# Convolution, then a squared-ReLU MLP, on one core: the plain-float32 part run once per 24 steps instead of once per 16

## The chip, the core and the metric

One core of a Trainium2 chip runs the whole program. Five engines take part: TensorE (PE, with its weight loads as PEld), VectorE (DVE), ScalarE (ACT), GpSimd (POOL) and SyncE (SP), which here only issues DMA transfers. Each engine has its own instruction stream and works through it in the order of the program; semaphores hold an instruction back until what it needs has happened on another engine. The metric is device time in microseconds (us) of one execution. A difference of less than about 0.2% can't be told from no change with the runs made here.

## The reference: what is computed

Input x has 8 sequences of 4096 tokens with 192 features. The first stage is a causal convolution with 7 taps per head (8 heads of 24 features), its taps a softmax of `weight`. The second is an MLP on 32768 tokens:

```python
out = np.einsum('hk,bskhg->bshg', w, x_unf)     # 7 taps, w = softmax(weight)
h = x @ w_in                                    # 192 -> 2048
r = np.maximum(h, 0.0)
g = s * (r * r) + b
return (g @ w_out).astype(np.float32)           # 2048 -> 192
```

## The kernel before, in words

Features lie on partitions and tokens along the rows. The 192 features are split: **A** is features 0 to 127, **B** the last 64. Of B, two blocks of 512 tokens are stacked on the 128 partitions.

**Tokens and steps.** Tokens go in groups of 1024, numbered n = 0 to 31; a group has two blocks j of 512. The hidden layer's 2048 units are 8 pairs p of 2x128. A *step* (n, j, p) computes one pair for one block. There are 512 steps, 16 per group; n = 0 and 1 run an older scheme (`OLD = 2`), the 480 steps of n = 2 to 31 the one that matters here.

**What a step does.** `first` (L549) makes h in PSUM: each operand is split into a high part of few bits and the rest, and three of the four products are taken, 18 matmuls of 64 rows, of which two run side by side on the two halves of the array. ACT applies Relu (L572) and Square (L580), which leaves the squares q in SBUF in float32. DVE makes the high part qh (L582) and the rest ql (L586). Two steps later (`LAG = 2`, the list `queue`) `second` (L717) multiplies qh and ql by the A columns of `w_out`, 12 matmuls, and accumulates over the 8 pairs. h has two buffers: the `first` of a step needs the Relu of the step two before.

**Features B.** The 64 B columns of the output are not made from qh and ql. The squares q are kept (`kept`, a ring of tiles named q), and once per group a *batch* makes them in plain float32: `second_B` (L736) runs, for each of the two blocks of the group before, 8 pairs x 4 matmuls of 64 rows and 64 columns, which run four at a time. The page counts each of them as two. After each block `evict_B` takes the result out:

```python
nc.scalar.activation(o, accs[0], ..., scale=sb, bias=...)       # L746, ACT, into oB
nc.scalar.activation(o2, accs[1], ..., scale=sb)                # L747, ACT, into oB2
nc.gpsimd.tensor_tensor(o, o, o2, op=ALU.add)                   # L748, POOL: first add
nc.sync.dma_start(oC, o[DB:P])                                  # L749, SP: upper half down
nc.gpsimd.tensor_tensor(oC, oC, o[0:DB], op=ALU.add)            # L750, POOL: second add
nc.sync.dma_start(outT[P:D, t0 : t0 + BLK], oC)                 # L751, SP: to HBM
```

The second add reads the lower half of oB; only after it may oB be written again. The tile `outs` has nine places: oA and oB rotate through three places each, oC, oB2 and oA2 have one. A is taken out likewise (L724 to L727), once per block.

**The convolution.** DVE does it for the group ahead, 7 instructions per piece of 128x512 (L174 and six times L176) for A of block 0, A of block 1 and B. `split_A` then makes the high part on ACT (L191), the rest on DVE (L193), and swaps the two 64-partition halves with two DMAs (L184, L185). `split_B` needs five DVE instructions and the same two DMAs. These are laid out as a stream of parts; `convolve(k)` puts the next k parts at its place in the program. Inputs of a group are loaded by two DMAs (xB L160, xA L163) into two buffers in turn; in the program they stand where the buffer's last reader has been issued, and the DMA waits on SP until that reader is done.

**What sets the order.** DVE, ACT and PE are held to the order in which the code issues them (`in_order`). SP and POOL too work through their streams in the order in which they stand in the program. So where a waiting DMA stands on SP, all DMAs behind it wait as well.

Of the kernel before, what the change touches and what calls it, by code (L numbers as in the profile page):

```python
# [17 lines left out]
P = 128  # L18
# [11 lines left out]
RING = 18  # L30

GAP = 40

FIRST = (3, 4, 2, 7)
# [11 lines left out]
def conv_attention_then_squared_relu_mlp(  # L46
# [96 lines left out]
    class Tokens:  # L143
        def __init__(self, n):
            self.n = n
            self.sA, self.wA = {}, {}
            self.todo = self.steps() if n else iter(())

            self.begun = False

        def load(self):
            n = self.n
            t0 = n * SUP
            self.xA = xin.tile([P, PAD + SUP], F32, name="xA")
            self.xB = xin.tile([P, PAD + BLK], F32, name="xB")
# [4 lines left out]
            nc.sync.dma_start(self.xB, xB[n])  # L160
            x0 = t0 - PAD
            cut = PAD + BLK if n == 0 else PAD + SUP
            nc.sync.dma_start(self.xA[:, skip:cut], xA[:, x0 + skip : x0 + cut])  # L163
            if n == 0:
                fetch(0, 0, CI)
                nc.sync.dma_start(self.xA[:, cut:], xA[:, BLK:SUP])

        def conv(self, acc, x, w, width):


            for k in range(K):
                src = x[:, k : k + width]
                if k == 0:
                    nc.vector.tensor_scalar(acc, src, w[:, 0:1], None, op0=ALU.mult)  # L174
                else:
                    nc.vector.scalar_tensor_tensor(  # L176
                        acc, src, w[:, k : k + 1], acc, op0=ALU.mult, op1=ALU.add
                    )
                yield k == K - 1
# [7 lines left out]
        def split_A(self, j, acc):  # L187

            s = self.sA[j] = xs.tile([P, 2, BLK], F32R, name="sA", bufs=3)
            self.wA[j] = xs.tile([P, 2, BLK], F32R, name="wA", bufs=3)  # L190
            nc.scalar.copy(s[:, 0, :], acc)  # L191
            yield
# [3 lines left out]
            self.swap(self.wA[j], s)  # L196
            yield

        def split_B(self, acc):

            self.tB = xs.tile([P, 2, BLK], F32R, name="tB")
            self.wB = xs.tile([P, 2, BLK], F32R, name="wB")
            hiB = xs.tile([P, BLK], F32R, name="hiB", bufs=1)
            nc.vector.tensor_copy(hiB, acc)
            yield
            for j in range(2):
                r = slice(j * DB, (j + 1) * DB)
                nc.vector.tensor_copy(self.tB[0:DB, j, :], acc[r, :])
                nc.vector.tensor_tensor(
                    self.tB[DB:P, j, :], acc[r, :], hiB[r, :].bitcast(F32), op=ALU.subtract  # L210
                )
                if j == 1:
                    self.swap(self.wB, self.tB)
                    self.begun = True
                yield

        def split_B_at_once(self, acc):

            self.tB = xs.tile([P, 2, BLK], F32R, name="tB")
            self.wB = xs.tile([P, 2, BLK], F32R, name="wB")  # L220
            hiB = xs.tile([P, BLK], F32R, name="hiB", bufs=1)
            nc.scalar.copy(hiB, acc)
            for j in range(2):
                r = slice(j * DB, (j + 1) * DB)
                places = (self.tB, self.wB) if j == 0 else (self.tB,)
                for k, to in enumerate(places):
                    nc.scalar.copy(to[k * DB :][0:DB, j, :], hiB[r, :].bitcast(F32))
                for k, to in enumerate(places):
                    nc.vector.tensor_tensor(
                        to[(1 - k) * DB :][0:DB, j, :], acc[r, :], hiB[r, :].bitcast(F32),  # L230
                        op=ALU.subtract,
                    )
                if j == 1:
                    self.swap(self.wB[:, 1, :], self.tB[:, 1, :])
                self.begun = True
                yield
# [9 lines left out]
        def half(self, j, i):  # L246
# [3 lines left out]
            b = (self.tB, self.wB) if i == 0 else (self.wB, self.tB)  # L250
# [3 lines left out]
                (2, b[0][r, j, :], b[1][r, j, :]),  # L254
            )

        def steps(self):
            for j in range(2):
                acc = xs.tile([P, BLK], F32, name="accA")
                yield from self.conv(acc, self.xA[:, j * BLK :], tapA, BLK)  # L260
                yield from self.split_A(j, acc)
                if j == 0:
                    acc = xs.tile([P, BLK], F32, name="accB", bufs=1)
                    yield from self.conv(acc, self.xB, tapB, BLK)
                    yield from (self.split_B_at_once if self.n == 1 else self.split_B)(acc)
# [7 lines left out]

        def finish(self, block):
            while not (block == 0 and self.begun) and next(self.todo, self) is not self:
                pass

# [80 lines left out]
    def fetch(p, a=0, z=None):  # L358
        if a == 0:
            k = 3 * (p % 3)  # L360
            room = outs[:, k : k + 3, :].rearrange("p a b -> p (a b)").bitcast(I32)
            words[p] = room.rearrange("p (f w) -> p f w", w=2)
# [5 lines left out]
    def room_for(dtype):  # L368
        return act.tile([P, 2, BLK], dtype, name="q")

    raw = [room_for(I32).rearrange("p a b -> p (a b)")[:, 0:CT] for _ in range(3)]
    splitB = [
        room_for(F32R).rearrange("p a (f k d) -> p (a f) k d", k=2, d=DB) for _ in range(2)
    ]
    scratch = room_for(F32)
    idle, ident = (scratch[:, k, 0:P] for k in range(2))
# [25 lines left out]
    def head():  # L402
# [11 lines left out]
        def diagonal(w):  # L414
            d = room_for(F32).rearrange("p a (k f) -> p (a k) f", f=P)
# [5 lines left out]
        diagB = diagonal(tapB)  # L421
# [3 lines left out]
        acc0 = xs.tile([P, BLK], F32, name="accA")  # L425
# [3 lines left out]
        diagA = diagonal(tapA)  # L429
        w0.magnitudes()  # L430
        split = one.split_A(0, acc0)
# [3 lines left out]
        tB = one.tB = xs.tile([P, 2, BLK], F32R, name="tB")  # L435
        wB = one.wB = xs.tile([P, 2, BLK], F32R, name="wB")
        hiB = xs.tile([P, BLK], F32R, name="hiB", bufs=1)
        lo = one.split_tensor(accB, hiB, lambda: one.conv_tensor(acc1, diagA, one.xA[:, BLK:], range(0, 2)))
# [6 lines left out]
        nc.scalar.copy(tB[top, 0, :], hiB[top].bitcast(F32))  # L445
        nc.scalar.copy(wB[bottom, 0, :], hiB[top].bitcast(F32))
        lo(tB[bottom, 0, :], top)
        lo(wB[top, 0, :], top)
# [5 lines left out]
        nc.scalar.copy(tB[top, 1, :], hiB[bottom].bitcast(F32))  # L454

        def second_block():
            sA = one.sA[1] = xs.tile([P, 2, BLK], F32R, name="sA", bufs=3)
            wA = one.wA[1] = xs.tile([P, 2, BLK], F32R, name="wA", bufs=3)
            lo1 = one.split_tensor(acc1, sA[:, 0, :])
            one.swap(wA[:, 0, :], sA[:, 0, :])  # L460
            lo(tB[bottom, 1, :], bottom)
            one.swap(wB[:, 1, :], tB[:, 1, :])
# [11 lines left out]
        start_tokens(1)  # L474
# [87 lines left out]

    def split_place(g):
        if g < OLD * 2 * NPAIR + LAG + 2 and g % DEEP > LAG:
            return room_for(F32R), room_for(F32R)
# [56 lines left out]
    def second_whole(n, j, p, qh, ql):  # L622
# [17 lines left out]
        if p == NPAIR - 1:  # L640
            t0 = n * SUP + j * BLK
            oA = out_tile("oA")
# [3 lines left out]
            oB = out_tile("oB")[0:DB]  # L646
# [7 lines left out]
    def second_split(n, j, p, qh, ql):  # L654
# [19 lines left out]
        if p == NPAIR - 1:  # L674
# [3 lines left out]
            o = {}  # L678
            own = None if early else room_for(F32)
            for k, name in ((1, "oB"), (0, "oA")):  # L680
                o[k] = out_tile(name) if early else own[:, k, :]
# [101 lines left out]
    def start_tokens(n):  # L783
        if n < NSUP:
            tok[n] = Tokens(n)
            tok[n].load()

    queue = []

    coming = [1]  # L790
# [3 lines left out]
    def convolve(k):  # L794


        k += owed[0]
        while k and coming[0] in tok:
            try:
                stop = next(tok[coming[0]].todo)  # L800
            except StopIteration:
                coming[0] += 1
                continue
            k -= 1
            if stop:
                break
        owed[0] = k if coming[0] in tok else 0
# [47 lines left out]
    steps = [(n, j, p) for n in range(NSUP) for j in range(2) for p in range(NPAIR)]  # L855

    def step(n, j, p):
        if p == 0:
            tok[n].finish(j)
            if j == 0:  # L860
                with headed():
                    start_tokens(n + 1)
            else:
                tok.pop(n - 1)
# [92 lines left out]
```

## Time and profile before

| what | value |
|---|---|
| median of 3 runs (lowest, highest) | 2223.55 us (2223.49, 2223.86) |
| profiled execution, its own time | 2223.51 us |
| its span from first to last instruction | 2221.7 us |
| PE busy / PEld busy | 2216.5 us (100%) / 1608.4 us (72%) |
| DVE busy / ACT busy / POOL busy | 1738.7 us (78%) / 1318.2 us (59%) / 302.6 us (14%) |
| granted PE clock | 1.00 |

The profile is of one execution, which took 1.8 us more than its span. A row of a timeline has the start in us from the span's start, the length, the engine, the line, what it writes and reads, its shape, and in brackets how long the engine stood idle before it and what ended that. "SPq" is the issue of a DMA, its landing comes later. A busy PE says little here, since matmuls overlap; the distance from one start to the next tells its pace.

### The profile page before, as it was taken

The numbers are of one execution on the slowest core, as the hardware profiler recorded it, in microseconds if no ns is written. First come the engines' busy times: TensorE is split into PE (matmuls) and PEld (weight loads), VectorE is DVE, ScalarE is ACT, GpSimd is POOL, SyncE is SP. The second block draws the span as 40 slices with busy tenths as digits, with TensorE's granted clock in tenths as the row PEclk, the third lists the DMA queues.
The fourth block names the chain that finished last, engine by engine and source line by source line (L and its number), as shares of the span: only waits on it lengthen the run. The fifth ranks groups of instructions, "written<-read, shape, count | busy, mean of one in ns | idle before, by whom it ended". The sixth has DMA issues, their size and how long they took to land.

```text
span 2221.7 us, 44630 instructions
## 1 busy us (share of the span) xinstructions
PE 2216.5 (100%) x19334; PEld 1608.4 (72%) x19334; DVE 1738.7 (78%) x1980; ACT 1318.2 (59%) x1424; POOL 302.6 (14%) x199
## 2 busy tenths in 40 slices
PE   9999999999999999999999999999999999999999
PEld 6788777777777777777877777777777777777776
DVE  8898787787877878778787777887787877878754
ACT  8758555566555665555655556555566555665554
POOL 0001111111111011111111101111111111011110
PEclk9999999999999999999999999999999999999999
DMA  5113212112121121211111111112112121121110
GB/s 181 33 34 95 57 48 61 48 47 58 44 58 48 44 58 44 58 51 51 48 54 49 53 50 47 53 49 63 46 46 58 44 58 49 46 56 39 44 30 17
DMA packets 46165, 117.49 MB, mean 53 GB/s; under 512 B 7760, under 2 KB 8016, under 8 KB 45968
## 3 DMA queue, kind: packets, MB, share of 16 engines
q1 hardware_dynamic: 45824, 114.50, 18.6%
q8 instruction: 151, 2.47, 0.5%
q14 instruction: 46, 0.38, 0.1%
q10 hardware_dynamic: 144, 0.13, 0.0%
HBM read 31.64 MB, written 25.17 MB: 26 GB/s over the span
## 4 chain that ended last, share of the span: by engine, by line
PE 98%; ACT 1%; DVE 1%; issue 0%; DVEq 0%; POOL 0%; POOLq 0%
PE h L549 47%; PE acc L717 29%; PE acc L736 18%; PE acc L661 2%; PE acc L270 1%; PE h L736 0%; ACT q L580 0%; PE acc L631 0%; PE acc L637 0%; PE acc L639 0%; PE acc L638 0%; ACT q L572 0%; PE acc L409 0%; DVE ql L586 0%; PE acc L630 0%; PE acc L633 0%
## 5 line engine op out<-in xcount | busy, mean ns | idle before, releaser
L572 ACT ACTIVATE q<-h 128x1024 f32<-128x1024 f32 x512 | 526.2, 1028 | 563.7 <-PE h L549 561.6
L586 DVE TENSOR_TENSOR ql<-q,qh 128x1024 fp32r<-128x1024 f32 x498 | 668.1, 1342 | 57.0 <-ACT qh L582 5.5
L582 DVE CAST qh<-q 128x1024 fp32r<-128x1024 f32 x482 | 342.5, 711 | 360.1 <-ACT q L580 356.3
L717 PE MATMUL acc<-qh,W 64*128 64x512 f32 x3816 | 588.1, 386 | 0.0
L580 ACT ACTIVATE q<-q 128x1024 f32<-128x1024 f32 x512 | 543.6, 1062 | 16.0
L549 PE MATMUL h<-sA,W 64*128 64x512 f32 x3072 | 436.1, 389 | 0.0
L549 PE MATMUL h<-wA,W 64*128 64x512 f32 x3072 | 431.9, 386 | 0.0
L549 PE MATMUL h<-wB,W 64*128 64x512 f32 x1536 | 430.3, 386 | 0.0
L549 PE MATMUL h<-tB,W 64*128 64x512 f32 x1536 | 430.3, 386 | 0.0
L717 PEld LDWEIGHTS acc<-qh,W 64*128 64x128 f32 x3816 | 357.4, 184 | 76.2 <-issue 0.8
L736 PE MATMUL acc<-q,WB 64*64 64x512 f32 x3776 | 412.1, 591 | 0.0
L717 PE MATMUL acc<-ql,W 64*128 64x512 f32 x1908 | 371.4, 386 | 0.0
L549 PEld LDWEIGHTS h<-sA,W 64*128 64x128 f32 x3072 | 285.1, 184 | 84.1 <-issue 24.7
L549 PEld LDWEIGHTS h<-wA,W 64*128 64x128 f32 x3072 | 287.8, 184 | 60.8
L736 PEld LDWEIGHTS acc<-q,WB 64*64 64x64 f32 x3776 | 141.5, 133 | 254.7 <-issue 254.7
L176 DVE SCALAR_TENSOR_TENSOR accA<-xA,tap,accA 128x512 f32<-128x512 f32 x378 | 312.9, 828 | 5.7
L549 PEld LDWEIGHTS h<-tB,W 64*128 64x128 f32 x1536 | 282.5, 184 | 41.1 <-issue 0.2
L549 PEld LDWEIGHTS h<-wB,W 64*128 64x128 f32 x1536 | 282.5, 184 | 20.4
L726 POOL TENSOR_TENSOR outs<-outs 128x512 f32<-128x512 f32 x59 | 95.4, 1617 | 1225.7 <-ACT outs L725 1225.7
L717 PEld LDWEIGHTS acc<-ql,W 64*128 64x128 f32 x1908 | 178.7, 184 | 37.7
L176 DVE SCALAR_TENSOR_TENSOR accB<-xB,tap,accB 128x512 f32<-128x512 f32 x186 | 167.5, 900 | 6.3
L748 POOL TENSOR_TENSOR outs<-outs 128x512 f32<-128x512 f32 x59 | 107.1, 1816 | 199.7 <-ACT outs L747 199.4
(146 smaller groups left out, 888.4 us busy)
## 6 DMA issues: line engine op xcount, KB each, us to landing
wA<-sA SPq DMA_DIRECT2D x126, 256.0 KB, 3.6
outT<-outs SPq DMA_DIRECT2D x62, 256.0 KB, 2.0
wB<-tB SPq DMA_DIRECT2D x60, 256.0 KB, 3.4
xA<-in_xA SPq DMA_DIRECT2D x24, 515.0 KB, 3.6
outT<-outs SPq DMA_DIRECT2D x65, 128.0 KB, 2.3
xB<-in_xB SPq DMA_DIRECT2D x32, 259.0 KB, 3.0
outs<-outs SPq DMA_DIRECT2D x60, 128.0 KB, 2.7
outs<-in_w SPq DMA_DIRECT2D x7, 768.0 KB, 6.1
```

The source lines that it names most:

```text
L176: nc.vector.scalar_tensor_tensor(acc, src, w[:, k : k + 1], acc, op0=ALU.mult, op1=ALU.add)
L270: nc.tensor.matmul(acc, diag[:, k, :], x[:, k : k + BLK], start=k == 0, stop=k == K - 1)
L549: nc.tensor.matmul(h[:, i, :], w_in(w, p, chunk[0], rows), chunk[part], start=start, stop=stop)
L572: nc.scalar.activation(q, h, AF.Relu)
L580: nc.scalar.activation(q, q, AF.Square)
L582: cast(qh, q)
L586: nc.vector.tensor_tensor(ql, q, qh.bitcast(F32), op=ALU.subtract)
L661: nc.tensor.matmul(accs[to + 2 * i][0:cols], w(f, r), q[r, f % 2, :], start=start and f == 0, stop=stop and f == NF - 1,)
L717: nc.tensor.matmul(accs[i], w(f, r), q[r, f % 2, :], start=f == 0 and lo == 0, stop=f == ends[i] and lo == 2,)
L726: nc.gpsimd.tensor_tensor(o, o, o2, op=ALU.add)
L736: nc.tensor.matmul(accs[r.start // HB][i * DB : (i + 1) * DB], WB[r, p, i, :], q[r, i, :], start=p == 0, stop=p == NPAIR - 1, skip_group_c ...
L748: nc.gpsimd.tensor_tensor(o, o, o2, op=ALU.add)
```

## The change

What it does, part by part:

- **Batches.** B is made once per 24 steps, three blocks at a time (`batch(k)`, `WINDOW`). 19 batches and three blocks in the last step take the place of 29 batches and two blocks in the last step. A batch stands at the second step of its 24 (`edge == 1`). At the first (`edge == 0`) the step's Relu is put off; Relu, Square, qh and ql of both steps come just ahead of the batch.
- **The ring of squares** is 12 tiles of two steps each (24 squares), before 18 tiles of one. The first Relu at a batch writes into a tile that the batch's first two pairs must have been read from.
- **SBUF.** To make room, `outs` has five places: oA, oB, oC, oB2 and oA2 have one each, none rotates. xA and xB have one buffer each, before two. The weights' staging area at the start lies in the ring.
- **B split as A.** `split` replaces `split_A` and `split_B`: one ACT and one DVE instruction for B too, and the halves' roles in `half` follow.
- **The convolution** is one stream (`pieces`) in the order B, A0, A1 per group. A split waits (`gated`) until the steps that read the buffer before it have been issued. One part per step goes in, 7 at edge 0, none at edge 1, and 5, 5 and 4 in the batch's three blocks. The next group's xB and xA are loaded right where the last tap of the present one is issued.

The order on three engines' queues at a batch, as the program has it. `Pool_49`, `PE_49`, `DVE_49` and `Activation_49` are the semaphores that POOL, PE, DVE and ACT raise, `DMAHW..` those of DMAs.

ACT before, from the Relu of the batch's step to that of the next (L724 and L725 take out A, L191 is a part of the convolution, L746 and L747 take out the two B blocks):

```order
L572 ACTIVATE q<-h 128x1024 [waits PE_49]
L580 ACTIVATE q<-q 128x1024 [waits Activation_49]
L724 ACTIVATE outs<-acc_9727,bias,sb 128x512 [waits DMAHW0_49,PE_49]
L725 ACTIVATE outs<-acc_9728,sb 128x512 [waits PE_49,Pool_49]
L191 CAST sA<-accA 128x512 [waits DMAHW3_49,DMAHW2_49,DVE_49]
L746 ACTIVATE outs<-acc_10030,bias,sb 128x512 [waits DMAHW4_49,PE_49]
L747 ACTIVATE outs<-acc_10031,sb 128x512 [waits PE_49]
L746 ACTIVATE outs<-acc_10076,bias,sb 128x512 [waits DMAHW0_49,PE_49]
L747 ACTIVATE outs<-acc_10077,sb 128x512 [waits PE_49,Pool_49]
L572 ACTIVATE q<-h 128x1024 [waits PE_49]
```

ACT in the changed kernel, the same place (L707 and L708 take out A, L555 is Relu, L563 Square, L214 a part of the convolution, L729 and L730 take out the three B blocks):

```order
L707 ACTIVATE outs<-acc_9138,bias,sb 128x512 [waits DMAHW6_49,PE_49,Pool_49]
L708 ACTIVATE outs<-acc_9139,sb 128x512 [waits PE_49]
L555 ACTIVATE q<-h 128x1024 [waits PE_49]
L563 ACTIVATE q<-q 128x1024 [waits Activation_49]
L555 ACTIVATE q<-h 128x1024
L563 ACTIVATE q<-q 128x1024 [waits Activation_49]
L214 CAST sA<-acc 128x512 [waits DMAHW4_49,DMAHW3_49,DVE_49]
L729 ACTIVATE outs<-acc_9439,bias,sb 128x512 [waits DMAHW0_49,PE_49]
L730 ACTIVATE outs<-acc_9440,sb 128x512 [waits PE_49]
L729 ACTIVATE outs<-acc_9487,bias,sb 128x512 [waits DMAHW0_49,PE_49,Pool_49]
L730 ACTIVATE outs<-acc_9488,sb 128x512 [waits PE_49,Activation_49]
L729 ACTIVATE outs<-acc_9532,bias,sb 128x512 [waits DMAHW2_49,PE_49,Pool_49]
```

The L729 of the second and third block now waits for `Pool_49`, which it did not before: the count that it waits for is that of the second add (now L733) of the block ahead of it, since oB has one place. Behind the third block's pair stands the next step's Relu.

SP before, at a batch (L184 and L185 swap the halves of a convolved block, L160 loads xB, L749 and L751 belong to the two B blocks):

```order
L184 DMA wA<-sA 64x1024 [waits DMAHW3_49,DVE_49,PE_49]
L185 DMA wA<-sA 64x1024 [waits DMAHW4_49]
L160 DMA xB<-in_xB 128x518 [waits DMAHW5_49,DVE_49]
L749 DMA outs<-outs 64x512 [waits DMAHW6_49,Pool_49]
L751 DMA outT<-outs 64x512 [waits DMAHW7_49,Pool_49]
L749 DMA outs<-outs 64x512 [waits DMAHW7_49,DMAHW0_49,Pool_49]
L751 DMA outT<-outs 64x512 [waits DMAHW1_49,Pool_49]
```

SP in the changed kernel at an odd batch (the first, third and so on; L190 and L191 swap, L168 loads xA, L732 and L734 belong to the B blocks):

```order
L190 DMA wA<-sA 64x1024 [waits DMAHW5_49,DVE_49,PE_49]
L191 DMA wA<-sA 64x1024 [waits DMAHW6_49]
L168 DMA xA<-in_xA 128x1030 [waits DMAHW7_49,DVE_49]
L732 DMA outs<-outs 64x512 [waits DMAHW0_49,Pool_49]
L734 DMA outT<-outs 64x512 [waits DMAHW1_49,Pool_49]
L732 DMA outs<-outs 64x512 [waits DMAHW2_49,DMAHW1_49,Pool_49]
L734 DMA outT<-outs 64x512 [waits DMAHW3_49,Pool_49]
L732 DMA outs<-outs 64x512 [waits DMAHW4_49,DMAHW3_49,Pool_49]
```

and at an even one (L172 loads xB):

```order
L172 DMA xB<-in_xB 128x518 [waits DMAHW3_49,DVE_49]
L732 DMA outs<-outs 64x512 [waits DMAHW4_49,Pool_49]
L734 DMA outT<-outs 64x512 [waits DMAHW5_49,Pool_49]
L732 DMA outs<-outs 64x512 [waits DMAHW6_49,DMAHW5_49,Pool_49]
L190 DMA wB<-sB 64x1024 [waits DMAHW7_49,DVE_49]
L191 DMA wB<-sB 64x1024 [waits DMAHW0_49]
L734 DMA outT<-outs 64x512 [waits DMAHW1_49,Pool_49]
L732 DMA outs<-outs 64x512 [waits DMAHW2_49,DMAHW1_49,Pool_49]
```

An input's load still stands ahead of the first block's downward DMA (L749 before, L732 now), in batches 1 to 18; in odd ones it is now xA, in even ones xB. In batch 19 nothing is left to load. On DVE, qh and ql of the two put-off steps stand ahead of the batch's parts; the load waits for the seventh tap of a block behind them: in odd batches seven taps and one split come between, in even ones six taps.

The core of the diff:

```diff
-RING = 18
+RING = 12
+BATCH = 24
+WINDOW = (5, 5, 4)
-FIRST = (3, 4, 2, 7)
...
-    outs = wide_w.tile([P, 9, BLK], F32, name="outs")
+    outs = wide_w.tile([P, 5, BLK], F32, name="outs")
-    xin = ctx.enter_context(tc.tile_pool(name="xin", bufs=2))
+    xin = ctx.enter_context(tc.tile_pool(name="xin", bufs=1))
...
+        def split(self, kind, j, acc):
+            s, w = self.places(kind, j)
+            nc.scalar.copy(s[:, 0, :], acc)
             yield
+            self.lo(s, acc)
+            self.swap(w, s)
             yield
...
     def room_for(dtype):
-        return act.tile([P, 2, BLK], dtype, name="q")
+        return act.tile([P, 2, 2, BLK], dtype, name="q")
...
     def relu(h):
         g = count[0]
         count[0] += 1
-        q = room_for(F32)
+        if g % 2 == 0:
+            two[0] = room_for(F32)
+        q = two[0][:, g % 2]
         nc.scalar.activation(q, h, AF.Relu)
         return q, g
...
-    room = {"oA": 0, "oB": 3, "oC": 6, "oB2": 7, "oA2": 8}
-    turn = {"oA": 0, "oB": 0}
+    room = {"oA": 0, "oB": 1, "oC": 2, "oB2": 3, "oA2": 4}
     def out_tile(name):
-        k = room[name]
-        if name in turn:
-            k += turn[name]
-            turn[name] = (turn[name] + 1) % 3
-        return outs[:, k, :]
+        return outs[:, room[name], :]
...
+    def pieces():
+        def whole(n, kind, j):
+            t = tok.setdefault(n, Tokens(n))
+            acc = xs.tile([P, BLK], F32, name="acc")
+            x = t.xB if kind == "B" else t.xA[:, j * BLK :]
+            for k, _ in enumerate(t.conv(acc, x, tapB if kind == "B" else tapA, BLK)):
+                if k < K - 1:
+                    yield None
+            with headed():
+                if kind == "B" and n + 1 < NSUP:
+                    tok[n + 1] = Tokens(n + 1)
+                    tok[n + 1].load_B()
+                elif j == 1 and n + 1 < NSUP:
+                    tok[n + 1].load_A(PAD + SUP)
+            yield "tapped"
+            gate = 16 * n - (0 if j else 8 if kind == "A" else 16)
+            while n + j > 1 and now[0] < gate:
+                yield "gated"
+            once = (n, kind) == (1, "B")
+            split = t.split_B_at_once(acc) if once else t.split(kind, j, acc)
+            next(split)
+            yield "after" if once else "cast"
+            next(split)
+            ready.add((n, kind, j))
+            yield None
...
-    def batch(n):
-        a = second_B(n, 0, banks())
-        convolve(FIRST[2])
-        evict_B(n, 0, a)
-        a = second_B(n, 1, banks())
-        convolve(FIRST[3])
-        evict_B(n, 1, a)
+    def batch(k):
+        for b, parts in zip(range(3 * k - 3, 3 * k), WINDOW):
+            block = OLD + b // 2, b % 2
+            a = second_B(*block, banks())
+            convolve(parts)
+            evict_B(*block, a)
+    def pace(g):
+        return 0 if g % BATCH < 2 else 1
...
+        g = now[0] - 16 * OLD
         h = first(n, j, p)
+        edge = g % BATCH if g >= BATCH else BATCH
+        if edge == 0:
+            convolve(4)
+            convolve(3)
+            second(*queue.pop(0))
+            waiting.append((n, j, p, h))
+            return
+        if edge == 1:
+            second(*queue.pop(0))
+            *at, before = waiting.pop()
+            put(*at, squares(before, nc.vector.tensor_copy))
...
         if (n, j, p) == steps[-1]:
-            a = second_B(n, 0, banks())
-            h = ps_h.tile([P, 2, BLK], F32, name="h")
-            b = second_B(n, 1, [h[:, i, :] for i in range(2)])
-            evict_B(n, 0, a)
-            last_B(n, 1, b)
+            a = second_B(n - 1, 1, banks())
+            evict_B(n - 1, 1, a)
+            for i in range(2):
+                h = ps_h.tile([P, 2, BLK], F32, name="h")
+                a = second_B(n, i, [h[:, k, :] for k in range(2)])
+                (last_B if i else evict_B)(n, i, a)
...
-        if n > OLD and (j, p) == (0, 1):
-            batch(n - 1)
+        if edge == 1:
+            batch(g // BATCH)
```

More of the change, by code (lines that the diff above doesn't have):

```diff
@@ L185, in swap, with places, lo @@
             nc.sync.dma_start(to[HB:P], of[0:HB])
[L187 to L192, printed above, removed]
+        def places(self, kind, j=0):
+            if (self.n, kind, j) == (0, "A", 0):
+                room = room_for(F32R)
+                s, w = room[:, 0], room[:, 1]
+            else:
+                s, w = (xs.tile([P, 2, BLK], F32R, name=x + kind) for x in "sw")
+            if kind == "A":
+                self.sA[j], self.wA[j] = s, w
+            else:
+                self.sB, self.wB = s, w
+            return s, w
+        def lo(self, s, acc):
             nc.vector.tensor_tensor(
@@ L217, in split_B_at_once @@
-        def split_B_at_once(self, acc):
[L219 to L236, printed above, removed]
+            self.lo(s, acc)
@@ L253, in half @@
                 (1 - i, self.wA[j][r, 0, :], self.wA[j][r, 1, :]),
-                (2, b[0][r, j, :], b[1][r, j, :]),
+                (2, b[r, 0, :], b[r, 1, :]),
             )
[L257 to L265, printed above, removed]
         def conv_tensor(self, acc, diag, x, taps=range(K)):
@@ L424, in head @@
         one.conv_tensor(accB, diagB, one.xB)
-        acc0 = xs.tile([P, BLK], F32, name="accA")
+        acc0 = xs.tile([P, BLK], F32, name="acc")
         for _ in one.conv(acc0, one.xA, tapA, BLK):
@@ L434, in head @@
         w0.his()
[L435 to L438, printed above, removed]
+        sB, wB = one.places("B")
+        lo = one.split_tensor(accB, sB[:, 0, :], lambda: one.conv_tensor(acc1, diagA, one.xA[:, BLK:], range(0, 2)))
         one.conv_tensor(acc1, diagA, one.xA[:, BLK:], range(2, K))
@@ L781, in last @@
             e.dma_start(outT[0:P, t0 + c.start : t0 + c.stop], oA[:, c])
[L783 to L786, printed above, removed]
     queue = []
-    coming = [1]
+    now = [0]
+    def pieces():
[23 more added lines that the diff above has]
+            yield None
+        order = [(1, "A", 0), (1, "B", 0), (1, "A", 1)]
+        for n in range(2, NSUP):
+            order += [(n, "B", 0), (n, "A", 0), (n, "A", 1)]
+        todo = [whole(*c) for c in order]
+        ahead = False
+        while todo:
+            said = next(todo[0], "over")
+            if said == "over":
+                todo.pop(0)
+                ahead = False
+                continue
+            if said in ("cast", "gated") and len(todo) > 1 and not ahead:
+                if said == "cast":
+                    yield said
+                said = next(todo[1])
+                ahead = said == "tapped"
+            yield said
+    ready = set()
+    stream = pieces()
     owed = [0]
@@ L797, in convolve, with need @@
         k += owed[0]
[L798 to L803, printed above, removed]
-            k -= 1
-            if stop:
-                break
-        owed[0] = k if coming[0] in tok else 0
+        owed[0] = 0
+        while k > 0:
+            said = next(stream, "over")
+            if said in ("over", "gated"):
+                return
+            k -= 1
+            if said == "tapped":
+                owed[0] = k
+                return
+    def need(*what):
+        while what not in ready:
+            if next(stream) == "gated":
+                raise ValueError(what)
     def pair(p):
@@ L873, in step @@
         else:
-            convolve(FIRST[p] if j == 0 and p < 2 else 1)
+            convolve(pace(g))
         if (n, j, p) == (2, 0, 0):
```

131 lines of the change are left out of this document (68 added, 63 removed).

## The prediction

> **What bounds the kernel now.** The page first: busy shares, then the chain of work that ended last.
>
> ```profile
> PE 2216.5 (100%) x19334; PEld 1608.4 (72%) x19334; DVE 1738.7 (78%) x1980; ACT 1318.2 (59%) x1424; POOL 302.6 (14%) x199
> ...
> PE 98%; ACT 1%; DVE 1%; issue 0%; DVEq 0%; POOL 0%; POOLq 0%
> ```
>
> PE is never free, and the chain is PE's own work to 98%. Everything else lies beside it. So a change can gain only by giving PE less time per token, and lose only by making PE wait. The pieces of that chain in order of time show the batches (first, a neighbour, the last with the two blocks of the last step):
>
> ```profile
> 905.06 13.89 PE acc L736 x128
> 973.62 13.89 PE acc L736 x128
> ...
> 2199.53 7.03 PE acc L736 x64
> 2206.56 6.87 PE h L736 x64
> ```
>
> A group of 16 steps takes 973.62 - 905.06 = 68.56 us. A block of B takes 6.87 (the second of the last step), and 0.16 more when it follows a step. Three stages, the batch, the step after it and the next one:
>
> ```profile
> 973.62:987.44 13.82, 13.82 (x128) 4.72 (x129) 12.71 (x15) 3.92 (x6) 2.97 (x2) 1.00 0.20 58
> 987.44:991.01 3.57, 3.57 (x34) 2.92 (x32) 1.03 (x2) 2.49 (x4) 0.00 (x0) 1.00 0.39 105
> 991.01:994.41 3.40, 3.40 (x32) 2.81 (x30) 2.31 (x2) 2.08 (x3) 2.19 (x2) 1.00 0.02 7
> ```
>
> An ordinary step is 3.40 us; the first after a batch is 3.57. 16 x 3.40 + 2 x 6.87 = 68.14, and 68.56 - 68.14 = **0.42 us is what one change to plain float32 and back costs**. PE has no other slack per group, and its clock stands at 1.00.
>
> **The change part by part.**
>
> *Fewer batches.* 29 batches become 19, the blocks stay 60: 10 x 0.42 = **-4.2 us**. The blocks in the last step are three and not two; the third moved there, its 6.87 us is in the sum anyway.
>
> *B split as A, one stream of parts, the new head.* Four DVE instructions fewer per group and one on ACT instead; they lie under PE. Cost 0, and no gain. One cover is thin: before every even batch a block's halves are swapped some 1.7 steps ahead of use. By my count of its Relu, Square, qh, ql and split its DMAs land about 0.2 us ahead of their matmuls; a late landing costs up to 1 us there. I take 0.
>
> *oB with one place.* This is where I expect the loss. How a block of B leaves the core, in the batch at 973.55, ACT, then SP, POOL and DVE:
>
> ```profile
> 981.67 0.77 ACT L746 ACTIVATE outs<-acc,bias,sb 128x512 f32<-128x512 f32 x1
> 982.35 0.68 ACT L747 ACTIVATE outs<-acc,sb 128x512 f32<-128x512 f32 x1
> 987.55 0.78 ACT L746 ACTIVATE outs<-acc,bias,sb 128x512 f32<-128x512 f32 x1 [4.52 <-PE acc L736]
> ...
> 989.85 1.03 ACT L572 ACTIVATE q<-h 128x1024 f32<-128x1024 f32 x1 [0.94 <-PE h L549]
> 990.91 1.06 ACT L580 ACTIVATE q<-q 128x1024 f32<-128x1024 f32 x1
> ```
> ```profile
> 988.53 0.33 SPq L160 DMA_DIRECT2D xB<-in_xB  x1
> 988.96 0.46 SPq L749 DMA_DIRECT2D outs<-outs  x1
> ```
> ```profile
> 983.10 1.70 POOL L748 TENSOR_TENSOR outs<-outs 128x512 f32<-128x512 f32 x1 [6.09 <-ACT outs L747]
> 992.22 1.62 POOL L750 TENSOR_TENSOR outs<-outs 64x512 f32<-64x512 f32 x1 [7.42 <-DMA outs<-outs]
> ```
> ```profile
> 981.80 0.69 DVE L193 TENSOR_TENSOR sA<-accA,sA 128x512 fp32r<-128x512 f32 x1 [0.68 <-ACT sA L191]
> 982.41 0.48 DVE L174 TENSOR_SCALAR accB<-xB,tap 128x512 f32<-128x512 f32 x1
> 982.92 5.58 DVE L176 SCALAR_TENSOR_TENSOR accB<-xB,tap,accB 128x512 f32<-128x512 f32 x6
> ```
>
> From L746 to the end of the second add, 993.84 - 981.67 = 12.17 us. The first add was done at 984.80, but its downward DMA went out at 988.96: on SP it stood behind the load of xB, which waited for DVE's last tap (982.92 + 5.58 = 988.50). In a batch with nothing to load, and at the very end, the same way is short:
>
> ```profile
> 2010.07 0.77 ACT L746 ACTIVATE outs<-acc,bias,sb 128x512 f32<-128x512 f32 x1
> ...
> 2015.75 1.51 POOL L750 TENSOR_TENSOR outs<-outs 64x512 f32<-64x512 f32 x1 [2.55 <-DMA outs<-outs]
> ```
> ```profile
> 2206.60 0.78 ACT L746 ACTIVATE outs<-acc,bias,sb 128x512 f32<-128x512 f32 x1 [4.90 <-PE acc L736]
> ...
> 2211.67 1.26 POOL L750 TENSOR_TENSOR outs<-outs 64x512 f32<-64x512 f32 x1 [2.37 <-DMA outs<-outs]
> ```
>
> 7.19 and 6.33 us. Before, the second block's L746 ran at 987.55 as soon as PE had the block, since oB rotated. Now it waits for the first block's second add, the third's for the second's, and behind the third on ACT stands the next Relu, for which PE waits. The places beside:
>
> ```profile
> 970.05 0.84 PE L549 MATMUL h<-sA,W 64*128 64x512 f32 x6
> ...
> 972.09 0.62 PE L717 MATMUL acc<-qh,W 64*128 64x512 f32 x4
> 972.55 0.39 PE L717 MATMUL acc<-ql,W 64*128 64x512 f32 x2
> ```
> ```profile
> 1009.01 0.69 DVE L582 CAST qh<-q 128x1024 fp32r<-128x1024 f32 x1 [0.31 <-ACT q L580]
> 1009.81 1.23 DVE L586 TENSOR_TENSOR ql<-q,qh 128x1024 fp32r<-128x1024 f32 x1
> ```
> ```profile
> xA<-in_xA SPq DMA_DIRECT2D x24, 515.0 KB, 3.6
> ...
> xB<-in_xB SPq DMA_DIRECT2D x32, 259.0 KB, 3.0
> ```
> ```profile
> DMA to landing us min/median/max: 2.2/2.6/4.9
> ```
>
> (The last row is that of L749.) Now a clock that starts with a batch's first float32 matmul, for the changed kernel:
>
> - The put-off Relu needs the tile of the first two pairs: 4 groups of four matmuls, 6.87/16 = 0.43 each, about 2.0. Relu, Square, Relu, Square: 2 x (1.03 + 1.06), to 6.1. DVE's qh and ql of the second: 0.69 + 1.23 and some 0.15 of gaps, to 8.2.
> - *Odd batches*: first tap 0.48, split 0.69, six taps 5.58 (with POOL's first add in them, as in the row): 14.9. xA's load goes out, L732 0.43 later (988.53 to 988.96). The add followed that by 3.26; xA is twice xB and lands 0.6 later: 3.9. The add itself, DVE soon idle, 1.4. The first block is out at 20.6.
> - *Even batches*: only six taps, 13.8; behind xB 0.43 + 3.3 + 1.4: 18.9.
> - The second block starts there (PE had it at 14.0) and takes 6.33 to 7.19; I take 6.8 in odd batches, and 7.2 in even ones, where taps and a swap run beside it. The third starts at 27.4 and 26.1. Its two ACT instructions take 1.36, the next Relu 1.03: done at **29.8 and 28.5**.
> - What PE needs: three blocks end at 0.15 + 20.61 = 20.76 on this clock (987.44 - 973.55 is 0.15 over two blocks), steps of 3.57 and 3.40 follow, so the third `first`, which needs that Relu's buffer, is due at 27.7, its `second` 2.04 and the first ql 2.50 later: 30.2. From the Relu's end to ql's end: 1.06 + 0.69 + 1.23 + gaps = 3.1. The Relu must end by **27.1**.
> - So PE loses 29.8 - 27.1 = 2.7 us in an odd batch, 1.4 in an even one, in two waits (first h, then ql). Batches 1 to 18: 9 x 2.7 + 9 x 1.4 = **+36.9**. Batch 19 has no load: twice 7.2 from 7.1 is 21.5, in time; 0.
>
> Sum: -4.2 + 36.9 = +32.7. The profiled execution took 2223.51 for a span of 2221.7, 0.04 from the median of 2223.55: **2256 us**.
>
> Bounds of the loss, which the trace of before doesn't contain. From below: taps without POOL's share (about 0.9 less), landings of 2.2, adds of 1.26 and second blocks of 6.33 give 26.6 in odd batches: nothing lost, -4.2 in all. From above: a landing of 4.9 and the second block at 7.6 (a slower add than 1.51) make some 4.4 and 3.0: +67. I stay near the middle, since the row behind a load (3.26) is the nearest there is.
>
> The Trainium skill ("DMA: Bandwidth & Descriptors", Issuing engines are not separate DMA queues) says that starting DMAs from several engines saves only the time to initiate them, small beside the transfer. By it the place behind a load on SP would cost 0.4 us, the first block would be out at about 14.5, and the sum would be -4.2. The row above disagrees: 4.16 us between the first add's end and its DMA, a wait of the issuing engine and no transfer.
>
> **The rivals.**
>
> - *A: the way out stays hidden* (not slower). If the first block is out by 18, or a short way makes up for it, the third L729 comes before 24.7 and PE never waits: 2223.5 - 4.2 = 2219.3. For it: 7.19 at 2010.07. Against: the load stands ahead of L732 in 18 of 19 batches, and seven taps can't end before 14.
> - *B: only odd batches wait.* Even ones have 1.4 to lose, one quick landing and an undisturbed add: 2223.5 - 4.2 + 9 x 2.7 = 2243.6.
> - *C: the clock falls.* If PE's wait of some 2 us at `first` makes the granted clock drop and a step then runs at half pace, each batch costs 3.4 more: 18 x 3.4 = +61, 2317. Against: the waits are short, and nothing in the row of 1.00 shows such a thing. The Trainium skill ("TensorE: Matmul & The Clock Gate", What's actually happening) puts the idle window after which the clock is halved at about 3.4 us; by it my 2.1 us would be safe, and no run shown here has a gap that tests it.
> - *D: the change gains more than the switch*, as DVE's and ACT's lighter load frees PE: with PE at 98% of the chain there is nothing to free; below 2219.
>
> **How the numbers follow.** The forecast, both kinds of batch waiting, 0.62; B and weaker forms of it 0.19; A 0.11; C 0.05; D 0.03. 0.2% is 4.4 us, the least that a measurement of this kernel can tell. A's -4.2 lies just inside it, so "same" gets A and a little of the weakest forms of B, 0.13; faster keeps D and A's luckier end, 0.05; slower 0.82. The likeliest case alone spans 2238 to 2275, by half to one and a half times its loss. The range takes in B and its weaker forms below, and a few more late landings above: 2226 to 2280; it leaves out A, C and D.
>
> **What would show it.** Right: 19 batches of about 20.8 us on PE; in 18 of them ACT idle ahead of the second and third L729, released by POOL's L733; PE waiting at the third step after a batch for ACT's L555, then for ql; L732 on SP right after a load; batch 19 without a wait; steps of 3.40 elsewhere. Wrong: PE in steps of 3.40 right through (A), waits in odd batches only (B), a granted clock under 1.00 (C), or waits at other places, such as wA's landing before even batches.

## The result, and the profile after

The changed kernel takes **2259.99 us** (median; 2259.81 to 2265.13) against 2223.52 beside it: a ratio of **1.0169**, 95% interval 1.0152 to 1.0187. It is slower by 1.7%. The forecast was 2256 us.

The page of the changed kernel, busy shares and the chain that ended last:

```profile
PE 2229.2 (99%) x19334; PEld 1616.9 (72%) x19334; DVE 1601.9 (71%) x1859; ACT 1323.9 (59%) x1449; POOL 274.7 (12%) x199
...
PE 77%; DVE 7%; ACT 6%; DMA 5%; POOL 3%; issue 2%; SPq 0%; DVEq 0%; POOLq 0%; ACTq 0%
```

PE is still busy for 99%, but the chain now leaves it for 23% of the span (before: 2%). That is what waits look like when each is short. The table of waits (who <- for whom: us in total, times, longest) names them:

```profile
ACT outs L729 <- POOL outs L733: 294.5, 37, 12.3
...
PE h L527 <- ACT q L555: 17.4, 10, 2.2
...
PE acc L700 <- DVE ql L569: 5.6, 16, 0.4
...
PE h L527 <- DMA wA<-sA: 0.6, 1, 0.6
```

19 batches have 38 second and third L729, and 37 of them wait for the add L733 (in batch 19 too, where it costs nothing). PE's own waits at the batches are the three rows below it: for a Relu, for ql, and once for a swapped half wA. An odd batch, the ninth, whose first float32 matmul starts at 1084.64; ACT, SP, POOL and PE in turn:

```profile
1091.77 0.78 ACT L729 ACTIVATE outs<-acc,bias,sb 128x512 f32<-128x512 f32 x1 [0.49 <-PE acc L719]
...
1105.31 0.78 ACT L729 ACTIVATE outs<-acc,bias,sb 128x512 f32<-128x512 f32 x1 [12.18 <-POOL outs L733]
...
1111.80 0.78 ACT L729 ACTIVATE outs<-acc,bias,sb 128x512 f32<-128x512 f32 x1 [5.13 <-POOL outs L733]
1112.48 0.68 ACT L730 ACTIVATE outs<-acc,sb 128x512 f32<-128x512 f32 x1
1113.05 1.02 ACT L555 ACTIVATE q<-h 128x1024 f32<-128x1024 f32 x1
```
```profile
1099.47 0.35 SPq L168 DMA_DIRECT2D xA<-in_xA  x1
1099.91 0.61 SPq L732 DMA_DIRECT2D outs<-outs  x1
```
```profile
1093.27 1.68 POOL L731 TENSOR_TENSOR outs<-outs 128x512 f32<-128x512 f32 x1 [5.77 <-ACT outs L730]
1104.01 1.26 POOL L733 TENSOR_TENSOR outs<-outs 64x512 f32<-64x512 f32 x1 [9.06 <-DMA outs<-outs]
```
```profile
1114.12 0.96 PE L527 MATMUL h<-sA,W 64*128 64x512 f32 x6 [1.59 <-ACT q L555]
...
1117.27 0.50 PE L700 MATMUL acc<-ql,W 64*128 64x512 f32 x2 [0.36 <-DVE ql L569]
```

Read it as one chain. L731 is done at 1094.95, its DMA L732 goes out only at 1099.91, right behind the load L168; the add L733 ends at 1105.27, and 0.04 later the second L729 starts. The third starts at 1111.80, the Relu behind it ends at 1114.07, and 0.05 later PE starts again. From one matmul start to the next there is 1.74 more than the usual distance at the first place and 0.52 at the second (the brackets count from modelled ends and show less).

An even batch (the tenth, from 1190.05) loses less; ACT and PE:

```profile
1208.75 0.78 ACT L729 ACTIVATE outs<-acc,bias,sb 128x512 f32<-128x512 f32 x1 [10.21 <-POOL outs L733]
...
1215.49 0.78 ACT L729 ACTIVATE outs<-acc,bias,sb 128x512 f32<-128x512 f32 x1 [4.88 <-POOL outs L733]
```
```profile
1217.82 0.96 PE L527 MATMUL h<-sA,W 64*128 64x512 f32 x6
...
1220.97 0.50 PE L700 MATMUL acc<-ql,W 64*128 64x512 f32 x2 [0.36 <-DVE ql L569]
```

The third `first` is on time; only ql is late. In batch 19, without a load, the third L729 starts at 2156.50, 22.4 after the batch's start, and PE waits nowhere.

From a batch's first float32 matmul to the next one's, 24 steps, three blocks and one switch should be 24 x 3.40 + 3 x 6.87 + 0.42 = 102.63 us. The trace has:

| batches | measured, us | over 102.63, each | sum |
|---|---|---|---|
| odd 1, 7, 9, 15, 17 | 105.33 to 105.69 | 2.70 to 3.06 | 14.1 |
| even 2 to 14, 18 | 103.29 to 103.80 | 0.66 to 1.17 | 7.9 |
| 3, 11 (granted clock falls) | 106.41, 106.67 | 3.78, 4.04 | 7.8 |
| 5, 13 (a swap of wA late behind them) | 106.51, 106.45 | 3.88, 3.82 | 7.7 |
| 16 (L732 lands after 4.98, not 3.1) | 105.55 | 2.92 | 2.9 |

Together 40.4. The span before less ten switches is 2221.7 - 4.2 = 2217.5, and 2217.5 + 40.4 = 2257.9, measured 2258.0. Nothing is left over.

### The profile page after: what moved, and what is told of

Same layout as the page of the kernel before. It is cut to its first block, busy times and chain, and to the rows that moved or that the text cites. A ratio compares the mean times of both kernels' runs of the same rounds, so it can differ in the third digit from the quotient of the medians.

```text
span 2258.0 us, 44538 instructions
## 1 busy us (share of the span) xinstructions
PE 2229.2 (99%) x19334; PEld 1616.9 (72%) x19334; DVE 1601.9 (71%) x1859; ACT 1323.9 (59%) x1449; POOL 274.7 (12%) x199
## 4 chain that ended last, share of the span: by engine, by line
PE 77%; DVE 7%; ACT 6%; DMA 5%; POOL 3%; issue 2%; SPq 0%; DVEq 0%; POOLq 0%; ACTq 0%
PE h L527 42%; PE acc L700 27%; PE acc L719 4%; DMA outs<-outs 4%; DVE acc L182 4%; ACT q L563 2%; ACT q L555 2%; POOL outs L733 2%; DVE ql L569 2%; PE acc L646 2%; DVE qh L565 1%; ACT outs L730 1%; POOL outs L731 1%; PE h L719 1%; PE acc L256 1%
## 5 line engine op out<-in xcount | busy, mean ns | idle before, releaser
L555 ACT ACTIVATE q<-h 128x1024 f32<-128x1024 f32 x512 | 525.0, 1025 | 437.2 <-PE h L527 428.1
L565 DVE CAST qh<-q 128x1024 fp32r<-128x1024 f32 x482 | 334.9, 695 | 486.5 <-ACT q L563 484.8
L569 DVE TENSOR_TENSOR ql<-q,qh 128x1024 fp32r<-128x1024 f32 x498 | 613.9, 1233 | 55.9 <-ACT qh L565 4.9
L563 ACT ACTIVATE q<-q 128x1024 f32<-128x1024 f32 x512 | 543.4, 1061 | 16.1
L527 PE MATMUL h<-sB,W 64*128 64x512 f32 x1536 | 431.6, 387 | 0.0
L719 PE MATMUL acc<-q,WB 64*64 64x512 f32 x3712 | 402.9, 590 | 0.0
L700 PE MATMUL acc<-ql,W 64*128 64x512 f32 x1908 | 378.6, 390 | 5.6 <-DVE ql L569 5.6
L527 PEld LDWEIGHTS h<-sA,W 64*128 64x128 f32 x3024 | 282.4, 184 | 95.4 <-ACT q L555 23.4
L182 DVE SCALAR_TENSOR_TENSOR acc<-xA,tap,acc 128x512 f32<-128x512 f32 x378 | 326.4, 864 | 6.8
L527 PEld LDWEIGHTS h<-sB,W 64*128 64x128 f32 x1536 | 283.1, 184 | 30.2 <-issue 0.2
L709 POOL TENSOR_TENSOR outs<-outs 128x512 f32<-128x512 f32 x59 | 99.6, 1688 | 1293.8 <-ACT outs L708 1293.8
L729 ACT ACTIVATE outs<-acc,bias,sb 128x512 f32<-128x512 f32 x58 | 45.2, 779 | 325.8 <-POOL outs L733 294.5
L182 DVE SCALAR_TENSOR_TENSOR acc<-xB,tap,acc 128x512 f32<-128x512 f32 x186 | 167.0, 898 | 3.6
```

The lines of the kernel that those rows point to most:

```text
L182: nc.vector.scalar_tensor_tensor(acc, src, w[:, k : k + 1], acc, op0=ALU.mult, op1=ALU.add)
L527: nc.tensor.matmul(h[:, i, :], w_in(w, p, chunk[0], rows), chunk[part], start=start, stop=stop)
L555: nc.scalar.activation(q, h, AF.Relu)
L563: nc.scalar.activation(q, q, AF.Square)
L565: cast(qh, q)
L569: nc.vector.tensor_tensor(ql, q, qh.bitcast(F32), op=ALU.subtract)
```

## The experiments

Theory: three things must meet. oB has one place; L732 is queued on SP behind a load that waits for DVE's last tap; and a Relu is queued on ACT behind the third L729. If so, undoing any one of them gives back the whole loss. Rivals are that one of them alone does it, or that PE waits for something else. Three kernels undo one each, and a fourth puts the one place into the kernel before.

**The load behind the way out.** In a batch the load is kept back in `put_off` until the block's eviction is written down, and put behind its last DMA on SP. The core of the edit:

```
+            in_batch[0] = True
             convolve(parts)
+            in_batch[0] = False
             evict_B(*block, a)
+            while put_off:
+                with behind(nc.sync):
+                    put_off.pop(0)()
```

> The changed kernel; only SP's order is touched: in a batch the load of xA or xB, which waits for DVE's last tap, stands behind the way out of the block instead of ahead of its L732. Theory (one place for oB, and L732 queued behind the waiting load): the first block is out at about 7.1 + 7.2 = 14.3 after the batch's first float32 matmul, the third L729 starts near 21.5, before 24.7, so PE waits nowhere: 2223.5 - 4.2 = 2219.3. Rival 1 (the one place alone does it, the load in front is beside the point): nothing gained, 2255 to 2260. Rival 2 (only a part of it is the load, the chains of three blocks stay too long): odd batches still lose about 1 us, 2228.

Measured 2220.60 us, ratio to the kernel before 0.9987 (0.9977 to 0.9996), granted clock 1.000. The ninth batch (from 1068.29), SP and ACT:

```profile
1078.74 0.55 SPq L732 DMA_DIRECT2D outs<-outs  x1
...
1091.16 0.54 SPq L168 DMA_DIRECT2D xA<-in_xA  x1
```
```profile
1083.65 0.78 ACT L729 ACTIVATE outs<-acc,bias,sb 128x512 f32<-128x512 f32 x1 [6.87 <-POOL outs L733]
...
1090.58 0.78 ACT L729 ACTIVATE outs<-acc,bias,sb 128x512 f32<-128x512 f32 x1 [5.57 <-POOL outs L733]
```

L732 goes out 10.4 after the batch's start and not 15.3. L729 still waits for L733 each time, but the third starts at 22.3, before 24.7. From batch to batch it is 102.63 fifteen times of eighteen (to within 0.02), as worked out from the rows before: the saving of 0.42 a switch is real. The rest, 1.7 us, is a swap of wA before batches 6, 12 and 14. The theory holds; rival 1 is out.

**Two places for oB**, every instruction left where it was:

```
-    outs = wide_w.tile([P, 5, BLK], F32, name="outs")
+    outs = wide_w.tile([P, 6, BLK], F32, name="outs")
...
-        o, o2, oC = out_tile("oB"), out_tile("oB2"), out_tile("oC")[0:DB]
+        o, o2, oC = outs[:, 1 + 4 * (j % 2), :], out_tile("oB2"), out_tile("oC")[0:DB]
```

> The changed kernel with a second place for oB, used in turn, and every instruction where it was; the load still stands ahead of L732. Theory: L729 of the second block no longer waits for the first block's second add; the third's place is the first block's, free at 20.6, when PE has the third block anyway (20.76); its Relu ends near 23.2, before 27.1. PE waits nowhere, 2219.3. Rival 1 (the late L732 alone does it): L732 still goes out at 15.3, so 2255 to 2260. Rival 2 (oC and oB2, which also have one place, take over as the next wait): second block's L732 waits for the first's way out, and at least the odd batches lose about 1 us: 2228.

Measured 2220.64 us, 0.9988 (0.9979 to 0.9998). The ninth batch (from 1068.14), SP and ACT:

```profile
1082.97 0.35 SPq L168 DMA_DIRECT2D xA<-in_xA  x1
1083.41 0.46 SPq L732 DMA_DIRECT2D outs<-outs  x1
```
```profile
1082.14 0.78 ACT L729 ACTIVATE outs<-acc,bias,sb 128x512 f32<-128x512 f32 x1 [5.51 <-PE acc L719]
...
1089.05 0.78 ACT L729 ACTIVATE outs<-acc,bias,sb 128x512 f32<-128x512 f32 x1 [5.56 <-PE acc L719]
```

L732 is as late as in the changed kernel (15.27 on the batch's clock), and nobody minds: L729 now waits for PE. oC and oB2 with their single places don't take over.

**The Relu ahead of the third eviction.** The third block's eviction is kept, and written down after the next step's Relu and Square:

```
             convolve(parts)
-            evict_B(*block, a)
+            if b % 3 == 2:
+                late_evict.append((block, a))
+            else:
+                evict_B(*block, a)
...
+        if edge == 2 and late_evict:
+            block, a = late_evict.pop()
+            evict_B(*block, a)
```

> The changed kernel; only ACT's order is touched: the third block's two evictions stand behind the next step's Relu and Square instead of ahead of them. Theory (PE waits since a Relu is queued behind the waiting third L729): that Relu ends near 23; the third L729 still starts near 27.3 in odd batches, and the Relu now behind it, due 3.40 later than the one before (30.5), ends at 27.3 + 1.36 + 1.03 = 29.7: no wait, 2219.3 to 2221. Rival (PE waits because its accumulators or the output's way are late, not for ACT's queue): the waits stay, 2250 or more.

Measured 2221.98 us, 0.9993 (0.9984 to 1.0002). The ninth batch (from 1067.85), ACT:

```profile
1088.14 0.78 ACT L729 ACTIVATE outs<-acc,bias,sb 128x512 f32<-128x512 f32 x1 [11.80 <-POOL outs L733]
...
1091.01 1.03 ACT L555 ACTIVATE q<-h 128x1024 f32<-128x1024 f32 x1 [1.52 <-PE h L527]
...
1095.04 0.78 ACT L729 ACTIVATE outs<-acc,bias,sb 128x512 f32<-128x512 f32 x1 [1.91 <-POOL outs L733]
...
1096.29 1.03 ACT L555 ACTIVATE q<-h 128x1024 f32<-128x1024 f32 x1
```

The third L729 is as late as ever (27.2 after the start), but the Relu for which PE waited has run, and the next one ends before it is due. It is 1 us over the forecast: in batch 16 L732 landed after 4.61 and the way to the next batch was 1.31 longer. There the second block's eviction is late, on ACT the cast of a split (L214) stands behind it, and on DVE five taps behind that; so the next qh starts at 1815.17, though its Square was done at 1812.30, and PE waits 0.9 for its ql. This path to PE goes by DVE and not by a Relu. The rest is the swap of wA again.

**One place in the kernel before**, 16 steps and two blocks a batch:

```
-        o, o2, oC = out_tile("oB"), out_tile("oB2"), out_tile("oC")[0:DB]
+        o, o2, oC = outs[:, room["oB"], :], out_tile("oB2"), out_tile("oC")[0:DB]
```

> The kernel before, 16 steps and two blocks a batch, with one part of the change alone: the blocks of B after the first steps have one place for oB instead of three in turn. Theory: the second block's L746 waits for the first block's second add (20.3 in most batches) instead of starting at 14.0; its two evictions and the next Relu end at 20.3 + 1.45 + 1.03 = 22.8, where 27.1 - 6.87 = 20.2 is due: 2.6 us in 25 batches with a load in front, 3.9 in the five of them whose way out took 1.3 longer: 2223.5 + 72 = 2295, or 2285 to 2305. Rival (only the larger batch makes the place short): 2223.5.

Measured 2283.31 us, 1.0274 (1.0256 to 1.0291). The one place costs more here than in the change, with 25 batches to pay in. The batch from 998.38, ACT and PE:

```profile
1018.08 0.78 ACT L746 ACTIVATE outs<-acc,bias,sb 128x512 f32<-128x512 f32 x1 [10.22 <-PE h L549]
1018.76 0.68 ACT L747 ACTIVATE outs<-acc,sb 128x512 f32<-128x512 f32 x1
1019.33 1.02 ACT L572 ACTIVATE q<-h 128x1024 f32<-128x1024 f32 x1
```
```profile
1020.40 0.97 PE L549 MATMUL h<-sA,W 64*128 64x512 f32 x6 [0.99 <-ACT q L572]
```

(The releaser in L746's bracket, PE, had long been done; the second add ended at 1018.04.) The mechanism is the expected one, the size was 12 us too large by the median, and 14 by the profiled execution, which took 2281.26 with the clock at 1.00 throughout (the other three took 2283.24 to 2285.99 at 0.999 to 0.997). I had put the first block out at 20.3, as in the kernel before. But with ACT held up DVE stands idle during the second add, which takes 1.28 and not 1.6, and most first blocks were out by 19.6 to 20.0; a batch lost 1.95 to 3.47. So the larger batch isn't what makes the place short.

**Where the clock falls.** In batches 3 and 11 of the changed kernel a wait of 2.0 and 2.1 us is followed by matmuls at half pace. Both stretches last 3.413 us, and their starts (485.08 and 1324.75) and the first record of the clock (7.21) are whole multiples of 3.413 apart: 140.00 and 246.00. So the clock seems to be set on a fixed grid. Two kernels lengthen the waits by repeating the third block's L730 once and twice (3 in place of the 2 in the second kernel):

```
-        nc.scalar.activation(o2, accs[1], AF.Identity, scale=sb)
+        third = (2 * n + j - 2 * OLD) % 3 == 2
+        for _ in range(2 if third else 1):
+            nc.scalar.activation(o2, accs[1], AF.Identity, scale=sb)
```

> The changed kernel with the eviction L730 of every third block done twice (0.68 us more on ACT ahead of the Relu for which PE waits). Theory for the time: each of 18 batches loses 0.68 more, +12. Theory for the clock, from the two drops seen: the granted clock is set anew on a fixed grid of 3.413 us, and a stretch of the grid with more than about 1.95 us of idle PE is followed by one at half clock; odd batches then wait 2.35 to 3.0 at the third step, and by chance of the grid about 5 or 6 of these 9 waits drop the clock, each costing some 1.2 net: 2260 + 12 + 4 = 2276. Rival 1 (every wait of over 2 us drops it): 9 or 10 drops, 2282. Rival 2 (the two drops had another cause): 2 or fewer, 2272.

> The same with the eviction done three times (1.36 us more). Time: 18 x 1.36 = 24.5 more. Clock: waits of 3.0 to 3.7 in odd batches, of which by the grid 7 or 8 of 9 drop it; even batches wait 1.3 and drop nothing: 2260 + 24.5 + 6.5 = 2291. Rival 1 (a wait of over 2 us always drops it): 9 or 10 drops, 2294. Rival 2 (another cause): 2 or fewer, 2284.

Measured, in one execution each, 2271.0 with 6 falls and 2286.1 with 7 (one of them two stretches long). Each has ten waits of over 2 us, of which four and three dropped nothing, so both rivals are out by the counts; by the times alone rival 2 would have been nearer. The 6 are as forecast. Of the 7, six are in odd batches, one fewer than the 7 or 8 forecast, and one is in batch 16, an even one, whose wait was 2.79 and not 1.3. These came 5 us short: the waits grew by 0.68 and 1.36 from a somewhat quicker base, and a fall costs less than 1.2: two batches with the same wait of 2.06 us, one with and one without, took 106.50 and 105.71, so 0.79, since at half pace the wait for ql goes away. Stretches of the grid around the limit, columns as in the table by stage above (PE busy second, clock third from the end), of the changed kernel, then of the two:

```profile
481.66:485.07 3.41, 1.56 (x14) 1.02 (x12) 0.00 (x0) 2.57 (x4) 1.88 (x2) 1.00 0.17 38
485.08:488.49 3.41, 3.41 (x18) 2.67 (x18) 2.53 (x3) 2.72 (x3) 1.04 (x2) 0.50 0.17 38
1846.95:1850.36 3.41, 1.68 (x16) 1.08 (x14) 1.37 (x2) 3.27 (x5) 1.34 (x2) 1.00 0.17 38
1850.37:1853.77 3.40, 3.04 (x26) 2.18 (x26) 3.21 (x3) 3.34 (x5) 1.40 (x1) 1.00 0.19 43
```
```profile
1117.54:1120.96 3.42, 1.52 (x14) 1.24 (x14) 0.40 (x1) 3.35 (x5) 1.27 (x1) 1.00 0.17 38
1120.97:1124.38 3.41, 3.41 (x18) 2.67 (x16) 3.31 (x4) 3.35 (x4) 1.47 (x1) 0.50 0.18 43
```
```profile
909.61:913.02 3.41, 1.70 (x16) 1.08 (x12) 0.00 (x0) 2.77 (x5) 0.54 (x1) 1.00 0.17 38
913.03:916.43 3.40, 2.49 (x22) 1.99 (x22) 1.31 (x2) 3.34 (x4) 1.27 (x1) 1.00 0.17 39
```

In these rows, where PE was busy for 1.56 or 1.52 us of 3.41, the next stretch ran at half clock; where for 1.68 or 1.70, at full clock. A wait of 2.31 us in batch 13 of the changed kernel did nothing, since the grid cut it in two.

**L732 started by POOL**, which has just made what it moves:

```
-        nc.sync.dma_start(oC, o[DB:P])
+        nc.gpsimd.dma_start(oC, o[DB:P])
```

> The changed kernel with the downward DMA of a block of B started by POOL, right behind the add that feeds it, and not by SP. Theory: it no longer stands behind the load; out at about 10.4 + landing 2.2 to 4.9 + 1.4 = 14 to 16.7 in odd batches, third L729 near 22 and below 24.7 unless starting it from POOL costs over 2 us a block more: 2219.3 to 2222. By the rule of the Trainium skill (DMA: Bandwidth & Descriptors, Issuing engines are not separate DMA queues), that another issuing engine saves only the time to initiate, at most 0.5 us a block: some 1 us of the 2.7 of an odd batch, 2240 to 2250. Rival: POOL's own start and descriptors are slow, and its adds wait behind them: 2260 or more.

Measured 2227.30 us, 1.0018 (1.0008 to 1.0028): most of the loss is gone, 7 us over the best stay. The first block is out at 15.3 in most odd batches. What stays comes of two more queues. The first batch (from 246.17), SP and POOL, and POOL in the third (from 451.45):

```profile
262.00 0.35 SPq L168 DMA_DIRECT2D xA<-in_xA  x1
262.43 14.85 SPq L734 DMA_DIRECT2D outT<-outs  x3
```
```profile
266.55 0.53 POOL L732 DMA_DIRECT2D outs<-outs  x1 [2.27 <-DMA outT<-outs]
...
466.30 0.38 POOL L166 MEMSET xA<- 128x6 f32 x1 [4.55 <-DVE acc L182]
466.81 0.53 POOL L732 DMA_DIRECT2D outs<-outs  x1
```

L734 is still behind the load on SP, and the second L732 needs the place that L734 empties: the third L729 comes at 23.4 to 25.0, which is just in time in most batches and costs 0.4 and 0.9 in two (8 and 7). In batches 3 and 11 POOL clears the edge of xA and waits for the same last tap as the load: L732 is as late as on SP (15.4), and these two batches lose 2.9 and 2.8. Another 0.9 and 0.3 are lost before batches 6 and 14, where the swap of wA is late in the changed kernel too.

**Every load behind the swap** of the split whose taps free its place, so that it is also ahead of no swap of wA (the second `next(split)` makes the low part and swaps):

```
-            with headed():
-                if kind == "B" and n + 1 < NSUP:
...
             next(split)
+            with behind(nc.sync):
+                if kind == "B" and n + 1 < NSUP:
...
```

> The changed kernel with every load of xA and xB from the second pair of blocks on put behind the swap of the split whose taps free its place, so that it stands ahead of no L732 in the batches and ahead of no swap of wA before the even ones. Theory: as with the load put off (2220.6, there 1.16, 0.42 and 0.11 us were still lost to a swap that landed late behind a load, after batches 5, 13 and 11) and without these: every batch to the next 102.63, 2223.5 - 4.2 = 2219.3. Rival 1 (the late swaps have another cause than the load ahead of them): 2220.6 as before. Rival 2 (the loads are now late for the taps): splits come late, 2222 or more.

Measured 2220.50 us, 0.9987 (0.9978 to 0.9996), in effect the same as with the load put off. The waits in the batches are gone again, but 0.90 us before batch 6, and 0.1 before 12 and 14, stay, with no load ahead. There the second half of the swap goes out 93.2 after the preceding batch's start, and its matmuls are due near 97.0; it landed at 96.9 where nothing was lost, and at 97.79 before batch 6. So it isn't the load; why that landing takes longer is open.

## Why the prediction was right, step by step

- *Fewer batches, -4.2.* Shown: 102.63 from batch to batch, without waits, is 24 steps, three blocks and one 0.42. With the waits at the batches gone, 2220.3 was measured for the profiled execution of the last kernel, and 1.2 of that is the late wA and gaps of 0.02: 2219.1 against 2219.3.
- *oB with one place, odd batches 2.7.* L732 at 15.27 (15.3), first block out at 20.6 to 20.9 (20.6), third L729 at 27.1 to 27.7 (27.4), Relu's end 29.4 to 30.0 (29.8). Undisturbed odd batches lost 2.8 on average.
- *Even batches 1.4.* Mis-sized: 0.99 on average in the eight undisturbed ones. The second block's way took 6.7 to 6.8 and not 7.2, and the first was out 0.2 to 0.5 earlier; the third L729 came at 25.2 to 25.5 (26.1), so only ql was late. The moment by which the Relu must end, 27.1, was about 0.4 too late: by it an even batch would have lost 0.6 and an odd one 2.4. PE's restarts (0.12 each) and the next ql (0.1 to 0.2) weren't in it.
- *Batch 19, 0.* So it was.
- *The thin cover of wA, taken as 0.* It broke before batches 6 and 14; 5 and 13 lost 1.2 and some 0.5 more than odd batches with the same wait at `first`. The bound of 1 us a place was about right; the term should have had 1.7 in all and not 0.
- *Rival C, the clock.* It happened, in 2 of 18 batches of the profiled execution and at about 0.8 us, not 3.4: half pace for 3.4 us loses 1.7, and part of it lay over a wait. "The waits are short" was no good reason against it: waits of 2.0 and 2.1 us were enough.
- *Rivals A, B and D* are out by the trace: all 18 batches with a load lose time, and nothing is gained beside the switches.
- In the sum (36.9 forecast, 40.4 measured) errors of both signs meet: batches 3 and 11 are 2.4 over the forecast (clock and longer waits), 5 and 13 2.3 (wA), 16 1.5 (its landing), the five undisturbed odd ones 0.6; the eight even ones 3.3 below. So the mechanism was right, but that the total came within 3.5 us is in part luck: the clock and wA, both put at nothing, happened to fill what the even batches fell short of.
- *The Trainium skill on issuing engines* ("DMA: Bandwidth & Descriptors", Issuing engines are not separate DMA queues): by its rule the place on SP was worth 0.4 us a block, and POOL as issuer was to give 2240 to 2250; 2227.3 was measured. What another engine saves here is a place behind a waiting instruction, 4.96 us in the ninth batch.

## What to carry to other kernels

Before a buffer loses its second place, follow the way out of what is in it, queue by queue: a DMA stands behind every earlier wait of the engine that starts it, and a Relu behind every earlier eviction. The loss here needed three things at once, the one place, the DMA behind a waiting load and the Relu behind a waiting eviction, and went away when any one of them was undone; the cheapest remedy was to write a load that has time behind an output that has none. The version so mended takes 0.9987 of the time before (0.9977 to 0.9996), where ten switches saved could give 0.9981; the rest went to the late swap of wA.

## What the runs showed of the hardware

The granted clock is set on a fixed grid of 3.413 us that runs through the whole program: in each of the three kernels with falls, all the stretches at half clock start whole multiples of it apart. How long PE stood still is measured here as the time from one matmul's start to the next, less the usual distance, and only the part inside one stretch counts. Over these three kernels, all 15 stretches up to the last step in which PE, at full clock, stood still for 1.91 us or more were followed by one at half clock, and none of those with 1.90 or less; so the limit lies at about 1.9. The profiles of two kernels without a fall agree: one place in the kernel before, and L732 started by POOL, have at most 1.85 in a stretch. It is the share within one stretch that counts and not the length of a wait: 2.31 us cut in two by the grid did nothing, 2.01 us inside one stretch did. In one case a stretch at half clock with another 0.73 us of waiting was followed by a second. The Trainium skill ("TensorE: Matmul & The Clock Gate", What's actually happening) has the free-running window and its length, 3413 ns, and the runs agree; it asks for an idle window before the clock falls, and here some 56% of one was enough.
